# A with K and B: one load and one set of transposes for each pair of chunks, and a new plan of the order

## The chip, the cores and the metric

The kernel runs on one core of a Trainium2 chip. The metric is device time in microseconds (us) of one execution, the median of three runs: 961.42 us before the change (956.11 to 964.44).

## The reference

Two things are computed one after the other: a recurrence over 768 steps with a 40 x 40 state for each of 4 x 8 heads, and an MLP across tokens and then across channels.

```python
B, H, S, D = 4, 8, 768, 40
for t in range(S):
    y[:, :, t] = einsum('bhd,bhde->bhe', r[t], state)
    Sa = einsum('bhde,bhe->bhd', state, a[t])
    state = state * w[t][:, :, None, :] - einsum('bhd,bhe->bhde', Sa, b[t]) \
            + einsum('bhd,bhe->bhde', v[t], k[t])
x = y.transpose(0, 2, 1, 3).reshape(B, S, H * D)
u = x + (relu(x.T @ w_tok1) @ w_tok2).T        # 768 -> 256 -> 768, each batch
out = u + relu(u @ w_ch1) @ w_ch2              # 320 -> 1536 -> 320
```

## The kernel before

The steps are cut into chunks of 64. A batch has 12 chunks, all of its 8 heads at once (two heads of a pair p lie in the two row halves of a tile), so there are 48 chunks, numbered through; most steps work on two neighbouring chunks, a chunk pair. The recurrence inside a chunk becomes a triangular system, which is solved, and the state goes from chunk to chunk through small matmuls.

- `t_prep`: a batch comes in four quarters of 16 steps of every chunk (`pin`, four loads of w, a, k, b). A scan (`CP`), a reciprocal (`rq`, `RC`) and some products give the decayed K, B, A and P, which are stored to DRAM as `sKB`, `sA` and `sP`.
- The A phase. `t_a` loads K and B of a chunk, all heads side by side, into `KBa` (two buffers) and A into `AT` (rows: head half and step); `t_a2` loads A of a chunk pair a second time, into the one buffer `A2`. Transposes on TensorE (`pk`, `pa`, helper L265) and copies give `KBT` and `ATB`, and `t_px` multiplies them (`px`, 16 matmuls a pair, L643) into the chunk matrices: `Dg`, `N21`, and the lower part of `AT`.
- `t_solve` (VectorE) inverts the 32 x 32 diagonal blocks of eight chunks at a time by steps of `tmp` and `Tl`, with results `TBt` and `TBn`; it runs six times. `merge` (`pm`) joins blocks, `t_b` (`pe`, `pt`, `ph`) makes `HU` of a pair.
- `t_load` and `t_v` bring v and r (`W2s`, transposed as `pv`), `t_chain` runs the recurrence (`pq`, `pr`, `pS`, `pU`: L1119, L1141, L1146, L1200 on), `t_y` the output (`yb`).
- `t_piece` cuts the MLP's weights into pieces (`cv_t` for the token weights, `cv_c` for the channel weights), splits each into two parts and stores them to `sT` and `sG`; `t_mlp` loads these (`wg`, on GpSimd's queue) and has five matmul stages a batch, m1 to m5 (L1638, L1528).
- While TensorE waits, `filler` (L358) multiplies an identity into a tile that nobody reads; 42 such matmuls stand at the start as a warm-up.

No loop order stands in the code. Each step is a generator that yields lists of instructions with an estimated duration, and `Planner` lays them out on a modelled clock: whenever an engine is free, the ready instruction of the lowest rank goes next, and fillers go where TensorE's modelled queue would idle. The ranks come from the table `K` (`a`, `prep`, `solve`, `mlp`, ...). The outcome is one fixed list for each engine, and on the chip every engine runs its list in order. A `Ring` hands out buffers: who needs one waits in the plan until it is given back, and on the chip the instruction waits for the last reader. The DMA queue of SyncE (SP) is such a list too: a load whose buffer is still in use holds up all loads behind it. Helpers record many operations under one line (L374 for most DMAs, L265 for transposes), so names are to be read with the lines.

Of the kernel before, what the change touches and what calls it, by code (L numbers as in the profile page):

```python
# [38 lines left out]
class Ring:  # L39
# [6 lines left out]
    @property  # L46
    def free(self):
        return not self.taken[self.given % self.n]
# [19 lines left out]
class Planner:  # L68
# [5 lines left out]
    TICK, ENTRY = 10240 / 3, 3300.0  # L74
# [22 lines left out]
    def rel(self, ring, now, slot=None):  # L97
        ring, slot = ring if isinstance(ring, tuple) else (ring, slot)
        ring.give(slot)
        while ring.queue and ring.free:  # L100
            ring.queue.sort(key=lambda x: (x[1][1], x[0]))
            _, t = ring.queue.pop(0)
            ring.take()
            self.step(t, max(t[2], now))

    def step(self, t, now):
        t[2] = now
        send = now
        while True:
# [17 lines left out]
            if isinstance(cmd, Ring):  # L127
                if not cmd.free or cmd.queue:
                    self.seq += 1
                    cmd.queue.append((self.seq, t))  # L130
                    return
                cmd.take()
                continue
# [22 lines left out]
    def clock(self, t0, ns, cols, form):  # L156
# [7 lines left out]
        return sw + (ns if self.cols.get(i - 1, 0.0) >= self.ENTRY else 2 * ns)  # L164

    def fill(self, t0):
# [14 lines left out]
        self.free["PE"] = now + self.clock(now, ns, 192.0, "A")  # L181
# [58 lines left out]
def tile_kernel(ctx, tc, r, k, v, w, a, b, wt1, wt2, wc1, wc2, out, dbg=None):  # L240
# [89 lines left out]
    sA = [tc.dram_tile([H, NC, C, D], F32, name=f"sA{i}") for i in range(B)]  # L330
# [16 lines left out]
    def bank(tag, shape, name):  # L347

        ring = PQ[tag]
        yield ring  # L350
        return ps.tile(shape, F32, tag=tag, name=name, bufs=K[tag]), (ring, ring.last)

# [32 lines left out]
    def t_prep(bi):  # L385
# [9 lines left out]
        for q in range(NQ):  # L395
# [10 lines left out]
            def load(i, src, q=q, d=d, ring=ring, tsl=tsl):  # L406
# [5 lines left out]
                return ("SP", (480.0, 683.0), f)  # L412

            def comp(q=q, d=d, ring=ring, tsl=tsl):
# [80 lines left out]
                def rest():  # L495
# [4 lines left out]
                    now = yield [dma(lambda: sKB[bi].rearrange("h c (w t) e -> (h c) w t e", w=2)[:, :, tsl], lambda: pin[:, 2:4], 650.0, 1365.0)]  # L500
# [9 lines left out]
                    dma(lambda: sA[bi].rearrange("h c t e -> (h c) t e")[:, tsl], lambda: A),  # L510
                    dma(lambda: sP[bi].rearrange("h c t e -> (h c) t e")[:, tsl], lambda: W)]
# [48 lines left out]
    R_at, R_kbt = Ring(ATN), Ring(2)  # L560
    R_kbas, R_atbs = [Ring(1) for _ in range(2)], [Ring(1) for _ in range(2)]
# [25 lines left out]
    ab_ready = [Event() for _ in range(NG)]  # L587
    R_a2 = Ring(1)

    def t_a2(g, rank):  # L590

        bi, c = divmod(g, NC)
        early = g < SETS[0]
        d = {}
        yield R_a2

        src = sA[bi].rearrange("(p h) c t e -> h c t p e", h=2)
# [3 lines left out]
        a2f = A2.rearrange("p h e -> p (h e)")  # L601

        def pa(p):
            def f():
                transp(d["pa"][0:DP, p, :], a2f[:, p * 128:p * 128 + DP], ident)
            return ("PE", (109, 256, "A"), f)
        for z in range(2):
            yield R_atbs[z]
        d["pa"], tk = yield from bank("c" if early else "w", [128, NP, 128], f"pa{g}")
        now = yield [pa(p) for p in range(NP)]  # L610
        P.rel(R_a2, now)

        def abc(z):
            o_, i_ = ATB[z], d["pa"][0:DP, :, z * 64:z * 64 + 64]
            if g < K["ea"]:
                return ("DVE", 420, lambda: nc.vector.tensor_copy(out=o_, in_=i_))
            return ("ACT", 380, lambda: nc.scalar.copy(out=o_, in_=i_))
        for z in range(2):
            now = yield [abc(z)]
            P.set(ab_ready[g + z], now)  # L620
        P.rel(tk, now)

    k_ready, x_done_ = [Event() for _ in range(NG)], [Event() for _ in range(NG)]

    def t_px(g, tag, rank):

        for z in range(2):
            yield ab_ready[g + z]
            yield k_ready[g + z]
        yield Dg_free[SETOF[g][0]]  # L630
        yield Dg_free[SETOF[g + 1][0]]
        bk = []
        for z in range(2):
            x = yield from bank(tag, [128, NP, 128], f"px{g + z}")
            bk.append(x)
# [1210 lines left out]
```

## Time and profile before

| What | Value |
|---|---|
| median of three runs | 961.42 us (956.11 to 964.44) |
| span of the profiled execution | 963.6 us |
| PE, matmuls | 846.3 us (88%), x14452 |
| PEld, weight loads | 761.9 us (79%) |
| DVE | 615.5 us (64%), x1533 |
| ACT | 530.9 us (55%), x1432 |
| POOL | 222.7 us (23%), x311 |
| DMAs on SP's queue by the program | 752, of which the A phase's loads are 240 |
| DMA bytes | 149.77 MB |

PE is busy for most of the span, but evenly only in its second half: the mean over the whole says little of where time can be won. A busy PE at a granted clock below 1 does its work at less than full speed. The DMA queue is shared by all loads and stores of SP; what counts there is which transfer an engine waits for.

### The profile page before, as it was taken

To read this page: it belongs to the slowest core of one execution; us is meant where nothing else is said; L and a number is where in the kernel's file an instruction comes from. 1 tells how busy PE (TensorE), PEld (TensorE's weight loads), DVE (VectorE), ACT (ScalarE), POOL (GpSimd) and SP (SyncE) were. 2 spreads that over 40 slices of the span, in tenths; PEclk is the share of its full clock that TensorE was granted. 3 is DMA by queue.
4 is the path that set the end of the run, shared out by engine and by line. 5 is a ranking of instruction groups with operands and counts; after the bars stand their busy time and mean duration, and the time that the engine had idled before them with its cause. 6 is when DMAs were issued, how large, how long until landed. Compare 5 with 4: busy or idle time off the path is not lost.

```text
span 963.6 us, 34457 instructions
## 1 busy us (share of the span) xinstructions
PE 846.3 (88%) x14452; PEld 761.9 (79%) x14452; DVE 615.5 (64%) x1533; ACT 530.9 (55%) x1432; POOL 222.7 (23%) x311
## 2 busy tenths in 40 slices
PE   2766756889989968699999999999999999999997
PEld 2655645768878857588889888999889898999997
DVE  7547767587757779457984489543895535354443
ACT  4255645677676757386677564556546445443221
POOL 6111236332534325131341011101121110000000
PEclk7888865577786778799999979999999999999999
DMA  7599776688776797937764937456337443255522
GB/s 204 149 178 197 170 185 173 182 200 191 189 184 154 177 253 194 227 65 172 183 176 76 232 97 190 93 130 146 75 97 215 136 120 75 81 138 154 181 90 86
DMA packets 271729, 149.77 MB, mean 155 GB/s; under 512 B 232528, under 2 KB 249680, under 8 KB 268496
## 3 DMA queue, kind: packets, MB, share of 16 engines
q1 hardware_dynamic: 265232, 100.31, 46.2%
q0 software_dynamic: 6336, 47.19, 15.1%
q8 instruction: 116, 1.90, 0.9%
q14 instruction: 45, 0.37, 0.1%
HBM read 113.05 MB, written 34.41 MB: 153 GB/s over the span
## 4 chain that ended last, share of the span: by engine, by line
PE 60%; DMA 14%; DVE 12%; ACT 5%; SPq 5%; issue 3%; POOL 0%; DVEq 0%; ACTq 0%; POOLq 0%
PE m L1528 17%; PE m L1638 14%; DMA KBa<-sKB 3%; PE pq L1146 3%; SPq L374 3%; PE pq L1119 2%; DMA cv_c<-in_moe_w_ch_dram 2%; PE pe L996 2%; PE pt L1025 2%; PE ph L1049 2%; DMA W2s<-in_r_dram 2%; PE pq L1141 2%; PE px L643 2%; PE yb L1261 2%; PE yb L1263 2%
## 5 line engine op out<-in xcount | busy, mean ns | idle before, releaser
L1638 PE MATMUL m<-ut,wg_c 128*128 128x256 f32 x1152 | 175.9, 294 | 2.3 <-DVE x L1678 2.2
L1638 PEld LDWEIGHTS m<-ut,wg_c 128*128 128x128 f32 x1152 | 150.9, 192 | 9.2 <-DVE x L1678 3.0
L1528 PE MATMUL m<-wg_c,hd 128*128 128x320 f32 x864 | 152.8, 320 | 1.6 <-DVE hd L1650 1.5
L1528 PEld LDWEIGHTS m<-wg_c,hd 128*128 128x128 f32 x864 | 129.9, 191 | 6.2 <-DVE hd L1650 2.6
L1648 ACT ACTIVATE hd<-m 128x256 fp32r<-128x256 f32 x144 | 55.4, 385 | 125.6 <-PE m L1638 124.2
L1650 DVE SCALAR_TENSOR_TENSOR hd<-m,hd 128x256 fp32r<-128x256 f32 x144 | 60.6, 422 | 79.6 <-ACT hd L1648 78.9
L1678 DVE TENSOR_TENSOR x<-m,x 128x320 f32<-128x320 f32 x96 | 46.8, 488 | 74.2 <-PE m L1528 73.9
L371 POOL TENSOR_TENSOR cv_c<-cv_c 128x320 f32<-128x320 f32 (+3 forms) x56 | 56.7, 1020 | 65.8 <-ACT cv_c L1364 51.7
L358 PE MATMUL yb<-ident 128*128 128x192 bf16 x530 | 67.0, 283 | 2.0 <-POOL ident masks.py:199 1.8
L728 ACT ACTIVATE Dg<-px 128x128 f32<-128x128 f32 x144 | 55.9, 388 | 22.8 <-PE px L643 14.5
L358 PEld LDWEIGHTS <-ident 128*128 128x128 bf16 x530 | 53.2, 113 | 7.2 <-POOL ident masks.py:199 1.8
L1463 POOL DMA_DIRECT2D wg_c<-sG x32 | 17.8, 556 | 158.0 <-PE m L1638 79.2
L371 POOL TENSOR_TENSOR pin<-pin,RC 96x640 f32<-96x640 f32 x18 | 32.2, 1796 | 91.7 <-DVE RC L479 53.6
L1155 POOL TENSOR_TENSOR RM<-G,upp 64x128 f32<-64x128 f32 x34 | 17.6, 526 | 152.5 <-ACT G L1136 143.5
L1261 PE MATMUL yb<-KB,RM 128*64 128x40 f32 x768 | 51.1, 238 | 0.0
L1263 PE MATMUL yb<-VSs,RBs 104*64 104x40 f32 x768 | 50.7, 237 | 0.0
L1235 ACT COPY VSs<-pU 40x160 f32<-40x160 f32 x88 | 25.1, 285 | 45.3 <-PE pU L265 44.1
L265 PE MATMUL pv<-ident,W2s 128*104 128x128 f32 x192 | 33.5, 294 | 16.6 <-DMA W2s<-in_r_dram 16.3
L265 PE MATMUL pk<-ident,KBa 128*104 128x128 f32 x192 | 36.3, 312 | 12.3 <-DMA KBa<-sKB 11.6
L1261 PEld LDWEIGHTS yb<-KB,RM 128*64 128x64 f32 x768 | 44.7, 148 | 0.6 <-issue 0.2
L1263 PEld LDWEIGHTS yb<-VSs,RBs 104*64 104x64 f32 x768 | 44.6, 147 | 0.0
L693 ACT COPY KBT<-pk 104x512 f32<-104x512 f32 x48 | 28.2, 587 | 27.5 <-PE pk L265 26.8
(203 smaller groups left out, 1979.0 us busy)
## 6 DMA issues: line engine op xcount, KB each, us to landing
wg_c<-sG POOLq DMA_DIRECT2D x16, 1152.0 KB, 6.1
wg_c<-sG POOLq DMA_DIRECT2D x16, 960.0 KB, 5.4
wg_t<-sT POOLq DMA_DIRECT2D x8, 1280.0 KB, 6.5
sKB<-pin SPq DMA_DIRECT2D x16, 480.0 KB, 4.0
KB<-sKB SPq DMA_DIRECT2D x48, 160.0 KB, 3.8
sG<-cv_c SPq DMA_DIRECT2D x24, 192.0 KB, 3.7
pin<-in_w_dram SPq DMA_DIRECT2D x16, 240.0 KB, 4.4
pin<-in_a_dram SPq DMA_DIRECT2D x16, 240.0 KB, 5.6
```

The lines of the kernel that those rows point to most:

```text
L265: nc.tensor.matmul(out_, lhsT=in_, rhs=idn, start=True, stop=True, is_transpose=True)
L358: nc.tensor.matmul(yb[:, 320:512], lhsT=zf[:, 0:128], rhs=zf[:, 0:192], start=True, stop=True)
L371: return [(e, Port(60 + f * n / 0.96 if e == "DVE" else 140 + 2.24 * n), lambda e=e: engines[e].tensor_tensor(out=out_(), in0=a_(), in1=b_ ...
L374: return ("SP", (ns, data), lambda: nc.sync.dma_start(out=dst(), in_=src()))
L728: return ("ACT", 190 if sl.start == 0 else 392, lambda: nc.scalar.activation(out=Dg[sl, :, ci * NP:(ci + 1) * NP].rearrange("p s n -> p n s"),
L1261: nc.tensor.matmul(dst, lhsT=rms[g - 1 + z][:, h, :], rhs=o["kb"][:, h, :], start=True, stop=False)
L1263: nc.tensor.matmul(dst, lhsT=o["rb"][:, h // 2, q0:q0 + 64], rhs=o["vs"][:, h // 2, 64:DP], start=False, stop=True)
L1528: nc.tensor.matmul(d[key], lhsT=lhs(i, a_), rhs=rhs(i, b_), start=i == 0 and j == 0, stop=i == n - 1 and j == 2)
L1638: nc.tensor.matmul(pt, lhsT=mm_[q][0], rhs=mm_[q][1], start=q == 0, stop=q == len(mm_) - 1)
L1648: nc.scalar.activation(out=hid[key][:, 0], in_=pt, func=AF.Relu)
L1650: now = yield [("DVE", dve(256), lambda: nc.vector.scalar_tensor_tensor(out=hid[key][:, 1], in0=pt, scalar=0.0, in1=hid[key][:, 0].bitcast ...
L1678: now = yield [("DVE", dve(320), lambda: tt(out=x()[:, i], in0=d[("c2", g, i)], in1=x()[:, i], op=ALU.add))]
```

## The change

A of a pair is loaded once. `t_a2`, `t_px` and the first half of `t_a` give way to `t_ab`, which handles a pair from its loads to `px`. K and B of both chunks go side by side into one buffer `KBp` of 128 x 8 x 2 x 64 (one buffer for two `KBa`), so a transpose of one head brings chunk z into row half z. A goes into a fixed tile of `AT` for the pair (six for thirteen single ones), of which a transpose takes heads q into column half q; `px` then takes its row half by the chunk and its column half by the head. A pair issues four DMAs, where it issued ten. `sA` is laid out with the chunk outermost, and the copy to `ATB` is one of 512 columns for a pair. Banks and ring slots can be taken two at a time (`banks`, `Ring.free(n)`). In the planner the estimated durations are written anew, and so are a few ranks of `K` and the price of a filler and of matmuls at the lower clock (`HALF`, `ENTRY`).

```diff
-K = dict(..., atn=13, ld=7.33, ..., slack_c=800, ..., b=1.98, ..., mrg=3.19, ..., warm=42, ..., prep=[-15.86, ...], ..., mlp=[11.7, 24.73, 34.3, 41.82], ...)
+K = dict(..., atn=6, kbp=1, ld=6.75, ..., slack_c=560.87, ..., b=2.06, ..., mrg=3.17, ..., warm=37, ..., prep=[-15.76, ...], ..., mlp=[11.72, 24.75, 34.32, 41.84], ...)
...
-    TICK, ENTRY = 10240 / 3, 3300.0
+    TICK, ENTRY = 10240 / 3, 3350.0
+    HALF = {"A": 1.93, "B": 1.85, "C": 1.92, "D": 1.05}
...
-        return sw + (ns if self.cols.get(i - 1, 0.0) >= self.ENTRY else 2 * ns)
+        return sw + (ns if self.cols.get(i - 1, 0.0) >= self.ENTRY else self.HALF[form] * ns)
...
-        self.free["PE"] = now + self.clock(now, ns, 192.0, "A")
+        self.free["PE"] = now + self.clock(now, ns, 236.0, "A")
...
-    KBa = zbufs([128, H, 64], "KBa", 2)
-    ATB = zbufs([DP, NP, 64], "ATB", 2)
-    A2 = zbufs([128, H, 64], "A2", 1)[0]
+    AW = DP + 128
+    KBp = zbufs([128, H, 2, 64], "KBp", K["kbp"])
+    ATs = [ctile([128, NP, AW], f"AT{i}") for i in range(ATN)]
...
-    sA = [tc.dram_tile([H, NC, C, D], F32, name=f"sA{i}") for i in range(B)]
+    sA = [tc.dram_tile([NC, H, C, D], F32, name=f"sA{i}") for i in range(B)]
...
-                return ("SP", (480.0, 683.0), f)
+                return ("SP", (520.0, 800.0), f)
...
-    def t_a2(g, rank):
...
-        yield [dma(lambda: A2[0:64, :, 0:D], lambda: sA[bi][:, c].rearrange("h s e -> s h e"), 480.0, 228.0)] + [
-            dma(lambda h=h: A2[64:128].rearrange("t (p h) e -> t p h e", h=2)[:, :, 1 - h, 0:D], lambda h=h: src[h, c + 1], 480.0, 114.0)
-            for h in range(2)]
...
+    def t_ab(g, rank):
...
+        yield prep_done[bi]
+        yield R_kbp
+        kbp = KBp[R_kbp.last]
+        yield R_at
+        at = ATs[R_at.last]
...
+        yield [dma(lambda z=z: kbp[:, :, z, 0:D], lambda z=z: sKB[bi][:, c + z].rearrange("h s e -> s h e"), 620.0, 960.0) for z in range(2)] + [
+               dma(lambda z=z: at[:, :, z * 64:z * 64 + D],
+                   lambda z=z: sA[bi][c + z].rearrange("(p q) t e -> (q t) p e", q=2), 655.0, 480.0) for z in range(2)]
...
+                    transp(pk[0:DP, h % 4], kbp[:, h].rearrange("p z e -> p (z e)")[:, 0:DP], ident)
...
+                transp(pa[0:DP, p], at[:, p, 0:DP], ident)
...
+            d["atb"] = ap_.tile([DP, NP, 128], F32, tag="ATB", name=f"ATB{g}", bufs=1)
...
                 for q in range(2):
                     for z in range(2):
-                        r0, c0 = q * 64, (q ^ z) * 64
-                        nc.tensor.matmul(bk[z][0][c0:c0 + 64, p, :], lhsT=ATB[z][r0:r0 + D, p, :],
-                                         rhs=st[g + z]["kbt"][r0:r0 + D, p, :], start=True, stop=True)
-            return ("PE", (250, 400, "C"), f)
+                        h = 2 * p + q
+                        nc.tensor.matmul(bk[z][0][q * 64:q * 64 + 64, p, :], lhsT=d["atb"][z * 64:z * 64 + D, p, q * 64:q * 64 + 64],
+                                         rhs=ks[h // 4][z * 64:z * 64 + D, h % 4, :], start=True, stop=True)
+            return ("PE", (218, 60, "C"), f)
...
     def t_a(g, rank):
...
-            yield [dma(lambda: kba[:, :, 0:D], lambda: sKB[bi][:, c].rearrange("h s e -> s h e"), 480.0, 910.0), lat(0), lat(1)]
...
-                return ("PE", (36, 16, "D"), f)
+                return ("PE", (16, 32, "D"), f)
...
-                return ("PE", (190, 832, "B"), f)
+                return ("PE", (178, 626, "B"), f)
...
+            if g % 2 == 0:
+                P.spawn(t_ab(g, ra), ra)
...
-            P.filler = (K["fill"] * 1e3, 80.0, K["fill_cols"], filler)
+            P.filler = (K["fill"] * 1e3, 83.0, K["fill_cols"], filler)
```

The order moves on every engine. On SP, right after the stores of the first batch's prep, the ten loads of the first pair stood ahead of the loads of the second batch's prep (`pin1`):

```order
L374 DMA A20_118<-sA0_156 64x8x40
L374 DMA A20_118<-sA0_156 64x4x40 x2
L374 DMA KBa0_110<-sKB0_152 128x8x40
L672 DMA AT0_441<-sA0_156 64x4x40 x2
L374 DMA KBa1_111<-sKB0_152 128x4x40 x2
L672 DMA AT1_470<-sA0_156 64x4x40 x2
L411 DMA pin1_0_479<-in_w_dram 96x640
L411 DMA pin1_0_479<-in_a_dram 96x640
L411 DMA pin1_0_479<-in_k_dram 96x640
L411 DMA pin1_0_479<-in_b_dram 96x640
```

In the changed kernel the pair has four loads there, and the four of `pin1_0`, the four of `pin1_1` and one of `pin1_2` follow, with the second pair's `KBp` behind them:

```order
L388 DMA KBp0_110<-sKB0_156 128x8x40 x2
L388 DMA AT0_112<-sA0_160 128x4x40 x2
L425 DMA pin1_0_454<-in_w_dram 96x640
L425 DMA pin1_0_454<-in_a_dram 96x640
L425 DMA pin1_0_454<-in_k_dram 96x640
L425 DMA pin1_0_454<-in_b_dram 96x640
L425 DMA pin1_1_468<-in_w_dram 96x640
L425 DMA pin1_1_468<-in_a_dram 96x640
L425 DMA pin1_1_468<-in_k_dram 96x640
L425 DMA pin1_1_468<-in_b_dram 96x640
L425 DMA pin1_2_490<-in_w_dram 96x640
L388 DMA KBp0_110<-sKB0_156 128x8x40 x2
```

Nine loads of the second batch's prep now stand between the first pair and the second.

On DVE the first solve starts with the transpose `DT0`. Before, the third quarter of the second batch's prep (`CP1_2`, `rq1_2`, `RC1_2`) was threaded through its first steps:

```order
L769 STREAM_TRANSPOSE DT0_935<-Dg0_120 128x32x32
L444 COPY D1_101<-CP1_1_740 96x40
L450 SCALAR_TENSOR_TENSOR CP1_2_962<-W1_102,D1_101 96x680
L791 TENSOR_TENSOR tmp0_1_979<-Tl0_107,DT0_935 128x2
L793 TENSOR_REDUCE Tl0_107<-tmp0_1_979 128x2
L791 TENSOR_TENSOR tmp0_2_985<-Tl0_107,DT0_935 128x8
L793 TENSOR_REDUCE Tl0_107<-tmp0_2_985 128x2x2
L464 TENSOR_SCALAR rq1_2_991<-ce1_545 96x80
L483 RECIPROCAL rq1_2_991<-rq1_2_991 96x80
L791 TENSOR_TENSOR tmp0_3_1003<-Tl0_107,DT0_935 128x18
L477 TENSOR_TENSOR RC1_2_1006<-rq1_2_991,CP1_2_962 96x2x40
```

Now a token weight's piece (`cv_t2_1_0`) and the copy of the fifth pair (`ATB8`) stand there:

```order
L748 STREAM_TRANSPOSE DT0_1080<-Dg0_124 128x32x32
L385 TENSOR_TENSOR pin1_3_578<-pin1_3_578 96x640
L770 TENSOR_TENSOR tmp0_1_1125<-Tl0_107,DT0_1080 128x2
L656 COPY ATB8_1127<-pa8_1096 104x512
L772 TENSOR_REDUCE Tl0_107<-tmp0_1_1125 128x2
L1333 TENSOR_SCALAR cv_t2_1_0_1005<-cv_t2_1_0_1005 128x384
L770 TENSOR_TENSOR tmp0_2_1142<-Tl0_107,DT0_1080 128x8
L1334 SCALAR_TENSOR_TENSOR cv_t2_1_0_1005<-cv_t2_1_0_1005 128x384
L772 TENSOR_REDUCE Tl0_107<-tmp0_2_1142 128x2x2
L1336 TENSOR_SCALAR cv_t2_1_0_1005<-cv_t2_1_0_1005 128x384
L770 TENSOR_TENSOR tmp0_3_1163<-Tl0_107,DT0_1080 128x18
```

The prep has gone ahead of the solve, and weight pieces, which need a load of their own, came in.

On PE the recurrence starts with `pq0` (the last of its first matmuls is the first row here), and `pq0 <- G0, HU0` is its second part. Before, px of the seventh pair (chunks 12 and 13) followed at once:

```order
L1119 MATMUL pq0_1_1923<-RBs0_136,VSs0_142 40x64
L947 MATMUL pm6_1816<-TBn0_1323,ET10_122 32x32 x9
L358 LDWEIGHTS ident_79
L358 MATMUL yb_166<-ident_79 128x192
L1141 MATMUL pq0_1_1923<-G0_895,HU0_1870 64x104 x4
L1141 MATMUL pq0_0_1922<-G0_895,HU0_1870 64x104 x4
L643 MATMUL px12_2011<-KBT12_1473,ATB0_114 64x128
L643 MATMUL px13_2012<-KBT13_1978,ATB1_115 64x128
```

Now the transposes of that pair (`pk12`) stand there, ahead of a filler:

```order
L1005 MATMUL pt2_2036<-ET2_1986,TBn0_1451 32x32 x5
L1115 MATMUL pq0_1_1981<-G0_686,HU0_1928 64x104 x4
L1115 MATMUL pq0_0_1980<-G0_686,HU0_1928 64x104 x4
L271 MATMUL pk12_0_1969<-ident_79,KBp0_110 104x128 x4
L372 LDWEIGHTS ident_79
L372 MATMUL yb_170<-ident_79 128x192
```

px of chunks 12 and 13 has moved behind the next chunk's pq. Counted over PE's whole list, fillers go from 530 to 693: from 416 to 503 ahead of pq0, from 79 to 167 between pq0 and the first matmul of the MLP (36 of them in one row just ahead of it), from 35 to 23 behind it.

## Rows read from the trace of the kernel before

**Rows 1.** Busy time by stretches of the span; columns in the first line.

```profile
core 0: us, PE busy (x) PEld busy (x) DVE busy (x) ACT busy (x) POOL busy (x), PEclk, DMA share, GB/s
0.00:41.00 41.00, 18.24 (x148) 17.80 (x149) 30.69 (x74) 17.13 (x25) 18.36 (x39) 0.75 0.67 192
41.00:163.00 122.00, 78.93 (x1390) 66.69 (x1390) 81.71 (x201) 63.90 (x134) 33.27 (x29) 0.77 0.77 172
163.00:373.00 210.00, 184.36 (x4048) 159.63 (x4045) 151.42 (x352) 143.66 (x383) 79.62 (x92) 0.72 0.79 195
373.00:600.00 227.00, 210.30 (x3641) 188.66 (x3637) 158.48 (x408) 141.68 (x401) 56.10 (x85) 0.94 0.66 155
600.00:870.00 270.00, 266.76 (x4554) 242.90 (x4544) 154.14 (x407) 142.30 (x425) 30.11 (x57) 1.00 0.47 121
```

**Rows 2.** Chain that ended last, in order of time: start us, us, what.

```profile
37.11 3.79 DMA sA<-pin
...
162.37 1.06 PE pq L1119 x30
...
373.39 3.14 PE m L1528 x20
```

**Rows 3.** Chain that ended last: shares by engine, then by line.

```profile
PE 60%; DMA 14%; DVE 12%; ACT 5%; SPq 5%; issue 3%; POOL 0%; DVEq 0%; ACTq 0%; POOLq 0%
...
by line: PE m L1528 17.0%; PE m L1638 13.6%; DMA KBa<-sKB 3.2%; issue 3.1%; PE pq L1146 2.7%; SPq L374 2.6%; PE pq L1119 2.4%; DMA cv_c<-in_moe_w_ch_dram 2.2%; PE pe L996 2.1%; PE pt L1025 2.0%; PE ph L1049 1.9%; DMA W2s<-in_r_dram 1.9%; PE
```

**Rows 4.** SP's queue in order of time: start us, us, what, how many.

```profile
40.92 1.98 SPq L374 DMA_DIRECT2D A<-sA  x3
42.94 0.61 SPq L374 DMA_DIRECT2D KBa<-sKB  x1
...
46.09 1.24 SPq L672 DMA_DIRECT2D AT<-sA  x2
```

**Rows 5.** Waits of SP's queue: us in total, times, longest us.

```profile
SPq L374 <- PE pk L265: 30.1, 10, 11.7
SPq L672 <- PE ph L1049: 24.1, 8, 9.4
...
SPq L374 <- PE pa L265: 18.9, 6, 10.6
```

**Rows 6.** DVE's timeline around the first solve; in brackets the idle time before.

```profile
99.94 0.42 DVE L616 COPY ATB<-pa 104x256 f32<-104x256 f32 x1 [3.14 <-PE pa L265]
...
105.94 0.20 DVE L464 TENSOR_SCALAR rq<-ce 96x80 f32<-96x80 f32 x1 [2.05 <-ACT ce L460]
...
130.81 1.99 DVE L450 TENSOR_TENSOR_SCAN CP<-W,D 96x680 f32<-96x680 f32 x1 [1.13 <-ACT W L433]
137.54 0.36 DVE L1359 TENSOR_SCALAR cv_t<-cv_t 128x384 int32<-128x384 int32 x1 [4.75 <-DMA cv_t<-in_moe_w_tok_dram]
137.82 0.27 DVE L959 TENSOR_TENSOR TBt<-pm,TBt 128x64 f32<-128x64 f32 x1
```

**Rows 7.** Groups of instructions by line: count | busy us, mean ns | idle before.

```profile
L358 PE MATMUL yb<-ident 128*128 128x192 bf16 x530 | 67.0, 283 | 2.0 <-POOL ident masks.py:199 1.8
...
L643 PE MATMUL px<-KBT,ATB 40*64 40x128 f32 x768 | 36.0, 319 | 6.6 <-ACT KBT L693 5.1 <-ACT PCt L535 1.5
```

**Rows 8.** PE's timeline: one run of px and one of pm.

```profile
78.60 1.42 PE L643 MATMUL px<-KBT,ATB 40*64 40x128 f32 x32
...
121.47 0.68 PE L947 MATMUL pm<-ET,TBn 32*32 32x32 f32 x32 [0.81 <-DVE ET L954]
```

**Rows 9.** PE's longest wait from 373 to 600 us: total, times, longest.

```profile
PE pv L265 <- DMA W2s<-in_r_dram: 8.0, 2, 7.7
```

**Rows 10.** DMA issues: count, KB each, median us from issue to landing.

```profile
sKB<-pin SPq DMA_DIRECT2D x16, 480.0 KB, 4.0
...
sA<-pin SPq DMA_DIRECT2D x16, 240.0 KB, 3.7
```

**Rows 11.** Chain from 250 to 373 us, shares by line.

```profile
by line: PE pq L1141 9.1%; DMA KBa<-sKB 8.7%; DMA cv_c<-in_moe_w_ch_dram 7.9%; issue 5.1%; PE yb L358 4.5%; PE pv L265 4.1%; PE pq L1119 4.0%; PE ph L1049 3.9%; DMA W2s<-in_r_dram 3.5%; DMA sG<-cv_c 2.8%; PE pe L996 2.7%; DMA P<-sP 2.7%; PE
```

More of the change, by code (lines that the diff above doesn't have):

```diff
@@ L44, in __init__, with free @@
         self.out = []
-    @property
-    def free(self):
-        return not self.taken[self.given % self.n]
+    def free(self, n=1):
+        return not any(self.taken[(self.given + i) % self.n] for i in range(n))
     def take(self):
@@ L99, in rel @@
         ring.give(slot)
-        while ring.queue and ring.free:
+        while ring.queue:
             ring.queue.sort(key=lambda x: (x[1][1], x[0]))
-            _, t = ring.queue.pop(0)
-            ring.take()
+            _, t, n = ring.queue[0]
+            if not ring.free(n):
+                return
+            ring.queue.pop(0)
+            for _ in range(n):
+                ring.take()
             self.step(t, max(t[2], now))
@@ L126, in step @@
                 continue
-            if isinstance(cmd, Ring):
-                if not cmd.free or cmd.queue:
+            if isinstance(cmd, (Ring, tuple)):
+                ring, n = cmd if isinstance(cmd, tuple) else (cmd, 1)
+                if not ring.free(n) or ring.queue:
                     self.seq += 1
-                    cmd.queue.append((self.seq, t))
+                    ring.queue.append((self.seq, t, n))
                     return
-                cmd.take()
+                for _ in range(n):
+                    ring.take()
                 continue
@@ L351, in bank, with banks @@
         return ps.tile(shape, F32, tag=tag, name=name, bufs=K[tag]), (ring, ring.last)
+    def banks(tag, shape, names):
+        ring = PQ[tag]
+        yield ring, len(names)
+        return [(ps.tile(shape, F32, tag=tag, name=n, bufs=K[tag]), (ring, (ring.last - len(names) + 1 + i) % ring.n)) for i, n in enumerate(names)]
     yb = ps.tile([128, 512], F32, tag="y", name="yb", bufs=1)
@@ L604, in f @@
             def f():
-                transp(d["pa"][0:DP, p, :], a2f[:, p * 128:p * 128 + DP], ident)
+                transp(pa[0:DP, p], at[:, p, 0:DP], ident)
             return ("PE", (109, 256, "A"), f)
-        for z in range(2):
[L608 to L635, printed above, removed]
+        yield [paf(p) for p in range(NP)]
@@ new lines, in atb @@
+        def atb():
+            d["atb"] = ap_.tile([DP, NP, 128], F32, tag="ATB", name=f"ATB{g}", bufs=1)
+            if g < K["ea"]:
+                nc.vector.tensor_copy(out=d["atb"], in_=pa[0:DP])
+            else:
+                nc.scalar.copy(out=d["atb"], in_=pa[0:DP])
+        now = yield [("DVE", dve(512), atb) if g < K["ea"] else ("ACT", act(512), atb)]
+        P.rel(tk, now)
+        for z in range(2):
+            yield Dg_free[SETOF[g + z][0]]
+        bk = yield from banks(tg[2], [128, NP, 128], [f"px{g}", f"px{g + 1}"])
@@ L684, in t_a @@
-        d = {}
-        def pk(p):
-            def f():
-                transp(d["pk"][0:DP, p, :], kbf[:, p * 128:p * 128 + DP], ident)
-            return ("PE", (109, 256, "A"), f)
-        def kbt():
-            d["kbt"] = ap_.tile([DP, NP, 128], F32, tag="KBT", name=f"KBT{g}", bufs=2)
-            nc.scalar.copy(out=d["kbt"], in_=d["pk"][0:DP])
-        yield R_kbt
-        d["pk"], tk = yield from bank(tg[0], [128, NP, 128], f"pk{g}")
-        yield [pk(p) for p in range(NP)]
-        now = yield None
@@ L1329, in t_piece @@
         yield A_loaded[min(K["conv_after"], NG - 1)]
-        ring = R_big if R_big.free and not R_wg.free and not mlp_on else R_wg
+        ring = R_big if R_big.free() and not R_wg.free() and not mlp_on else R_wg
         yield ring
```

158 lines of the change are left out of this document (73 added, 85 removed).

## The prediction

> **What bounds the kernel now.** The table by stretches comes first, because a mean over 963.6 us hides three regimes [rows 1]. Up to 41 us TensorE has almost nothing to do (18.24 us busy). [...] From 373 to 600 us it is 210.30 of 227 us busy at 0.94, and from 600 us to 870 it is 266.76 of 270 at 1.00: there only a cheaper matmul shortens anything. So time can be won ahead of 373 us, where the first MLP matmuls start [rows 2], and little after it. The chain that ended last says the same: 60% PE, but 14% DMA landings, 12% DVE and 5% SP's issuing [rows 3], and the last three lie mostly in the first 373 us.
>
> Next, the SP queue in order of time. From 40.92 to 47.33 us it does nothing but issue the ten loads of the first chunk pair, at about 0.6 us each [rows 4]. Then the waits of that queue: it stood 18.9 us for pa to free the one A2 buffer, 30.1 us for pk to free KBa and 24.1 us for ph to free AT [rows 5]; each time every load behind it stood as well. Last, DVE's own timeline around the first solve: it idles 3.14 us ahead of an ATB copy, 2.05 us ahead of rq, 1.13 us ahead of the scan of prep 2 and 4.75 us ahead of a weight piece [rows 6]. That last wait holds a merge's TBt, so the recurrence, whose first pq runs at 162.37 us [rows 2].
>
> **The change part by part.**
>
> *SP issues.* Ten DMAs per pair become four (two KBp, two AT): 6 x 24 = 144 of 752 issues go, and A crosses once instead of twice (160 KB less per pair, 3.84 of 149.77 MB). At 0.6 us that is 86 us of the queue's time, 50 us of it ahead of the MLP (14 of 24 pairs). Most of this isn't on the path. The chain gives SP 5% of 963.6 us = 48 us; with 144/752 = 19% of the issues gone the proportional share is 9 us. Ends: 0 if what follows on SP waits for buffers anyway, and 25 us, the whole 2.6% that the chain books on the loads' helper line L374 [rows 3]. I take **-9**, because the order puts other work in the gap: the eight loads of prep 1's first two quarters and W2s come forward to where A2 and AT stood, so KBp of the second pair still queues behind nine 240 KB loads.
>
> *DVE around the first solve.* Before, prep 1's third and fourth quarter are threaded through the solve; now they are done ahead of it and five weight pieces (cv_t) are threaded through instead. The stalls of [rows 6] between 96 and 138 us are 3.14 + 2.05 + 1.13 + 4.75 = 11.1 us. If all vanish, -11; if the pieces inside the solve wait for their loads as the one at 137.54 did, two such waits cost +10. I take **-5**: about half goes, since the merges no longer have a fresh load just ahead of them, while ATB of the fifth pair still waits for its KBp inside the solve.
>
> *px.* The same 16 matmuls per pair, but the row half now changes at every matmul (z picks the row, q the column), where two neighbours shared it. 36.0 us in all [rows 7]. No row shows this shape in the new order. Ends: 0, and the pace of the merges' matmuls, which step through the row groups: 0.68 against 1.42 us for 32 records [rows 8], hence 36.0 x (1 - 0.68/1.42) = 19 us less, for a quarter of the columns. The diff writes 218 for 250 into the plan, 13%; I take that, **-4.6**, much nearer to zero since px streams 128 columns. [...]
>
> *Landings that PE waits for after 373 us.* pv waits 8.0 us in two pieces for W2s [rows 9]. In the new order pv of chunk 17 stands behind the first three MLP tiles and pq16 instead of ahead of them, so W2s has that much longer to land. Ends 0 and -8; **-3**, as other loads still share the queues with the big weight loads.
>
> *The store of A.* sA's layout puts chunks outermost, so the store's destination reads 8x12x640 where it was 96x640. The last such store of prep 0 lies on the chain for 3.79 us [rows 2]. Ends 0 and +3.8 (all of it twice); sKB with twice the bytes lands in 4.0 against 3.7 us [rows 10], so bytes are a small part: **+0.3**. [...]
>
> *Fillers.* 530 become 693 by the order: 87 more before pq0, 88 more between pq0 and the first MLP matmul (79 before), 12 fewer after it. Each is 67.0/530 = 0.126 us of PE [rows 7]. The first 87 fall in a stretch where PE idles 122 - 79 = 43 us [rows 1] and cost nothing while it does; 11 us stand if that cover is gone. Of the 88, at most 11 us are on the path; before, fillers were 4.5% of the chain from 250 to 373 us [rows 11], 5.5 us or half of what they took there. Against that stands a higher clock in a stretch that has 0.72. Ends: +11 and -25 (last rival). I take **+3**.
>
> *At nothing:* the five fewer memsets and six small new ones (GpSimd, before 41 us, under prep 0's DMA and DVE work); 24 ATB copies of 512 columns for 48 of 256 (ACT is 143.66 of 210 us busy, and idle enough afterwards); five fewer warm-up matmuls, in a stretch where PE waits 20 us; AT's ring of 12 chunks for 13, since the second batch's first pair waits for ph of the first pair either way. If ACT or that ring were the last to be waited for, each would show as one wait of the sort in [rows 5], 1 to 3 us.
>
> Sum: -9 - 5 - 4.6 - 3 + 0.3 + 3 = -18.3 us, and 963.6 - 18.3 = 945.3 us. The profiled execution lies 2.2 us above the median of the three runs (961.42; 956.11 to 964.44), so the forecast is 945.3 - 2.2 = **943 us**, and its own range, with the middle halves of the bounds, 933 to 953.
>
> **The rivals.**
>
> *Washed out, 958 us.* The front gets shorter but the first MLP matmul doesn't start sooner, because it waits for weight pieces and x0, and the recurrence runs behind in the in-order queue of PE. For it: 36 fillers stand in one row just ahead of that matmul, a place where the plan itself expects to wait. Against: the pieces come earlier in SP's order than before. Left are px and W2s: 961.4 - 4.6 - 3 + 3 = 957, say 958.
>
> *Slower, 973 us.* DVE stalls inside the first solve. Five pieces stand between its steps; the last ones can be loaded only after an earlier piece is stored and its buffer given back, and SP issues that store in order behind AT and prep 1's stores. Each such wait is a 4.75 us one, and the whole recurrence (pq0) is behind it. Three waits in the first solve give +14, and TBt reaches pe late. It decides from the second wait on: with one, the stalls that go still pay for it. 961.4 + 14 - 4.6 - 3 + 5 (no stall gained, some fillers on the path) = 973. For it: the wait at 137.54 us was of this kind. Against: the pieces start earlier.
>
> *The clock, 922 us.* The fillers hold the clock up from 163 to 373 us. At the 0.94 of the next stretch, 184.36 us of PE work would be 184.36 x 0.72/0.94 = 141 us, plus 11 us of fillers: 32 us less, bounded by DVE's 151 us and the chain of ACT and DVE between the matmuls, so about -25. Then 961.4 - 25 - 14 (SP and DVE terms) = 922. Against: in that stretch 79 fillers did not do it, and half of the added ones stand in two rows of 13 and 16 and one of 36.
>
> **How the numbers follow.** Forecast 0.50, washed out 0.23, slower 0.17, clock 0.10. Range 922 to 973: it leaves out a tenth at either end, roughly. The three runs of the kernel before span 0.9%, so 1% is about what a measurement can tell from no change. Faster by over 1% means under 951.8: most of the forecast's case (0.46) and the clock's (0.10), 0.56. Slower by over 1%, over 971.0: most of the slower case and the tail of the second, 0.17. The rest, 0.27, is within.
>
> **What would show it.** Right: SP's timeline from 41 to 100 us with gaps; no wait for pa on SP; pq0 at 150 to 157 us; the first MLP matmul at 355 to 362 us; px under 32 us in all; after 600 us PE as busy as now. Wrong: pq0 at 162 us or later, waits of DVE for cv_t between the solve's steps, or the first MLP matmul at 370 us again in spite of an earlier pq0 (then the weights set it); a clock over 0.85 from 163 to 373 us would speak for the last rival. What I can't read from the trace is how the many small waits of five in-order queues add up under a new order; that alone can move the time by the 1% either way.

## The result and the profile after

The changed kernel took 946.88 us (median of five runs, 946.75 to 954.88) against 962.90 for the kernel before (956.11 to 971.50, also five): a ratio of 0.987, 95% interval 0.983 to 0.991. The forecast was 943 us with a range of 922 to 973. The profiled execution was the slowest of the five (span 953.2 us), so a second profile of the same kernel (span 947.7 us; run `same_again` below) is read beside it wherever a few us count.

Starts of the first matmul of a stage, read from the three traces (us):

| | before | after | again |
|---|---|---|---|
| first ph | 151.2 | 151.2 | 148.6 |
| pq of chunk 0, first part | 162.3 | 156.1 | 153.1 |
| pq of chunk 0, second part (needs G and HU) | 164.2 | 162.0 | 159.4 |
| first MLP block | 373.3 | 361.3 | 357.5 |
| second | 578.7 | 560.4 | 553.9 |
| third | 737.9 | 726.8 | 719.0 |
| fourth | 875.6 | 864.9 | 858.7 |

So the first part of pq0 runs 6 to 9 us earlier, 12 to 16 us are won by the first MLP block and 6 to 9 more by the second; 6 to 7 of them are given back ahead of the third. Of the 6 to 9 us, some 4 are only a matter of order: the first part now stands ahead of other matmuls, and the second part, without which the recurrence doesn't go on, comes 2 to 5 us earlier. PE's timeline before, after and again:

```profile
164.17 3.04 PE L1141 MATMUL pq<-G,HU 104*64 104x104 f32 x16
```

```profile
161.99 3.03 PE L1115 MATMUL pq<-G,HU 104*64 104x104 f32 x16
```

```profile
159.40 3.04 PE L1115 MATMUL pq<-G,HU 104*64 104x104 f32 x16
```

The stretches of [rows 1] in the profile after (columns as there):

```profile
0.00:41.00 41.00, 16.64 (x130) 16.25 (x131) 31.95 (x74) 17.12 (x25) 19.30 (x41) 0.71 0.65 181
41.00:163.00 122.00, 86.45 (x1631) 76.55 (x1629) 82.72 (x208) 67.97 (x140) 50.10 (x41) 0.81 0.82 196
163.00:373.00 210.00, 186.56 (x4155) 160.01 (x4153) 155.97 (x370) 149.76 (x392) 74.61 (x85) 0.85 0.73 182
373.00:600.00 227.00, 213.32 (x3723) 188.83 (x3725) 153.49 (x408) 139.09 (x389) 49.17 (x73) 0.96 0.64 150
600.00:870.00 270.00, 262.87 (x4394) 239.91 (x4395) 147.43 (x396) 139.39 (x418) 29.61 (x56) 0.99 0.47 120
```

PE is about as busy in each of them; its clock from 163 to 373 us is 0.85 instead of 0.72. That looks like the last rival, and an experiment has to tell whether it is. After 600 us PE now idles 7 us where it idled 3.

The groups of [rows 7], the chain's shares by engine [rows 3] and its landing of the A store [rows 2], in the same profile:

```profile
L372 PE MATMUL yb<-ident 128*128 128x192 bf16 x693 | 80.7, 274 | 3.8 <-DVE P L1267 2.0 <-POOL ident masks.py:199 1.8
...
L670 PE MATMUL px<-KBT,ATB 40*64 40x128 f32 x768 | 31.1, 301 | 12.4 <-DVE ATB L656 6.1 <-DVE rq L478 2.7 <-DVE fl L560 2.7
```

```profile
PE 59%; DMA 14%; DVE 12%; issue 6%; ACT 6%; SPq 3%; POOL 0%; DVEq 0%; ACTq 0%; POOLq 0%
```

```profile
38.25 5.53 DMA sA<-pin
```

px takes 31.1 us for 36.0, SP's issues 3% of the chain for 5%, fillers 80.7 us for 67.0, and the store of A lands in 5.53 us where it took 3.79. SP's queue in order of time [rows 4]:

```profile
42.14 1.03 SPq L388 DMA_DIRECT2D KBp<-sKB  x2
43.79 1.05 SPq L388 DMA_DIRECT2D AT<-sA  x2
44.89 0.49 SPq L425 DMA_DIRECT2D pin<-in_w_dram  x1
...
50.05 1.78 SPq L388 DMA_DIRECT2D KBp<-sKB  x2
51.88 5.79 SPq L388 DMA_DIRECT2D AT<-sA  x2
```

The first pair costs 2 us of the queue where it cost 6. The second pair's two AT issues take 5.79 us, though (5.41 in `same_again`). What holds them isn't shown: the issue right behind, of 240 KB at 57.71 us, took 0.50 us again. SP's waits for ph to free AT, over the whole span:

```profile
SPq L388 <- PE ph L1029: 48.5, 6, 28.5
```

The waits for pa are gone, but those for ph have doubled (24.1 us before, 9.4 at the longest [rows 5]; 40.6 in `same_again`), and 31 of the 48.5 us lie between the first and the second MLP block. DVE around the first solve [rows 6]:

```profile
80.36 0.36 DVE L1333 TENSOR_SCALAR cv_t<-cv_t 128x384 int32<-128x384 int32 x1 [3.86 <-DMA cv_t<-in_moe_w_tok_dram]
...
99.80 1.96 DVE L748 STREAM_TRANSPOSE DT<-Dg 128x1024 f32<-128x1024 f32 x1
...
126.21 0.36 DVE L1333 TENSOR_SCALAR cv_t<-cv_t 128x384 int32<-128x384 int32 x1 [0.79 <-issue]
...
127.78 1.96 DVE L826 STREAM_TRANSPOSE TBt<-Tl 128x1024 f32<-128x1024 f32 x1
```

The weight pieces inside the solve hardly wait (under 1 us each), and the merges have no stall of 4.75 us. But the solve starts at 99.80 us, 14 us later than before (85.7), since prep's third and fourth quarter stand ahead of it, and the first ph runs at the same 151 us. What is won inside the solve is lost again by its later start.

### The profile page after: what moved, and what is told of

Read it like the earlier page. It is cut to its first block, busy times and chain, and to the rows that moved or that the text cites. A ratio compares the mean times of both kernels' runs of the same rounds, so it can differ in the third digit from the quotient of the medians.

```text
span 953.2 us, 34564 instructions
## 1 busy us (share of the span) xinstructions
PE 843.6 (89%) x14605; PEld 758.2 (80%) x14605; DVE 607.1 (64%) x1538; ACT 531.0 (56%) x1412; POOL 227.0 (24%) x304
## 4 chain that ended last, share of the span: by engine, by line
PE 59%; DMA 14%; DVE 12%; issue 6%; ACT 6%; SPq 3%; POOL 0%; DVEq 0%; ACTq 0%; POOLq 0%
PE m L1502 15%; PE m L1612 13%; DMA W2s<-in_r_dram 4%; PE pm L927 3%; SPq L388 3%; PE pq L1095 2%; PE pq L1120 2%; PE pt L1005 2%; PE pv L271 2%; PE ph L1029 2%; DMA cv_t<-in_moe_w_tok_dram 2%; PE yb L372 2%; PE px L670 2%; PE pq L1115 2%; PE pe L976 2%
## 5 line engine op out<-in xcount | busy, mean ns | idle before, releaser
L372 PE MATMUL yb<-ident 128*128 128x192 bf16 x693 | 80.7, 274 | 3.8 <-DVE P L1267 2.0
L372 PEld LDWEIGHTS <-ident 128*128 128x128 bf16 x693 | 66.1, 109 | 10.0 <-issue 4.0
L271 PE MATMUL pv<-ident,W2s 128*104 128x128 f32 x192 | 32.9, 289 | 19.5 <-DMA W2s<-in_r_dram 16.9
L970 POOL COPY TBD<-TBt 32x256 f32<-32x256 f32 x33 | 22.2, 673 | 111.2 <-PE ph L1029 85.8
L1235 PE MATMUL yb<-KB,RM 128*64 128x40 f32 x768 | 48.0, 230 | 0.0
L385 POOL TENSOR_TENSOR pin<-pin,RC 96x640 f32<-96x640 f32 x19 | 33.8, 1787 | 59.4 <-DVE RC L493 38.1
L1237 PE MATMUL yb<-VSs,RBs 104*64 104x40 f32 x768 | 47.6, 229 | 0.0
L271 PE MATMUL pk<-ident,KBp 128*104 128x128 f32 x192 | 35.2, 301 | 12.3 <-DMA KBp<-sKB 12.3
L1235 PEld LDWEIGHTS yb<-KB,RM 128*64 128x64 f32 x768 | 40.8, 137 | 1.7 <-issue 0.8
```

The costliest lines, as they stand in the source:

```text
L271: nc.tensor.matmul(out_, lhsT=in_, rhs=idn, start=True, stop=True, is_transpose=True)
L372: nc.tensor.matmul(yb[:, 320:512], lhsT=zf[:, 0:128], rhs=zf[:, 0:192], start=True, stop=True)
L385: return [(e, Port(60 + f * n / 0.96 if e == "DVE" else 140 + 2.24 * n), lambda e=e: engines[e].tensor_tensor(out=out_(), in0=a_(), in1=b_ ...
L1235: nc.tensor.matmul(dst, lhsT=rms[g - 1 + z][:, h, :], rhs=o["kb"][:, h, :], start=True, stop=False)
L1237: nc.tensor.matmul(dst, lhsT=o["rb"][:, h // 2, q0:q0 + 64], rhs=o["vs"][:, h // 2, 64:DP], start=False, stop=True)
```

## The experiments

Three sets of four kernels; each set ran beside the kernel before on one chip, six to twelve executions of each kernel. A time is the median; a ratio is to the kernel before, with its 95% interval. Traces are of one execution each: pq0 and the MLP blocks are read from it, and a few us between two traces can be chance.

**1. same_again**: the changed kernel, no edit.

> The changed kernel once more, unchanged. Its profiled execution took 8 us more than the other four, and in it TensorE idled 8 us from 560 to 727 us, behind a load of x. If that wait was a matter of one execution, a second profile shows 945 us and the load of x ends no wait. If it is in the order, it is there again and the time is 947 all the same. Either way 945 to 949 us.

949.08 us, 0.987 (0.982 to 0.992). The wait is there again, in the chain of waits of this profile:

```profile
690.74 8.24 DMA sX<-P
699.00 5.61 DMA x<-sX
704.63 0.47 ACT sp L1462
```

and in its waits of PE from 554 to 719 us:

```profile
PE pU L271 <- ACT VSs L1209: 4.0, 1, 4.0
```

So it belongs to the order: x of a batch goes through DRAM, ACT's next instruction in order waits for it, and the copies to VSs of the recurrence stand behind that. The kernel before had no such wait (PE idled 3 us from 579 to 738 us; 8 us here from 554 to 719).

**2. no_mid_fill**: the changed kernel without the 167 fillers between pq0 and the first MLP matmul; all other instructions in the same order.

```diff
+FILL0, FILL1 = 503, 670
...
+    nfill = [0]
+
     def filler():
+        nfill[0] += 1
+        if FILL0 < nfill[0] <= FILL1:
+            return
         nc.tensor.matmul(yb[:, 320:512], lhsT=zf[:, 0:128], rhs=zf[:, 0:192], start=True, stop=True)
```

> The 167 fillers between pq0 and the first MLP matmul are left out, all else in the same order. Theory of the clock: the granted clock of that stretch falls from about 0.83 to the 0.72 of before or lower, the stretch grows by 6 us or more, and the time is 953 to 962 us. Theory that fillers are load without use: 19 us less work for TensorE there, half of it on the path, 936 to 942 us. If they only fill gaps: 945 to 949 us at an unchanged clock.

951.36 us, 0.987 (0.982 to 0.991), the same as with them. The stretch from pq0 to the first MLP block of this kernel:

```profile
156.00:360.00 204.00, 170.53 (x4009) 146.99 (x4001) 145.67 (x360) 146.28 (x387) 74.54 (x83) 0.77 0.77 185
```

and of `same_again`:

```profile
153.00:358.00 205.00, 176.56 (x4195) 151.83 (x4184) 144.48 (x359) 147.49 (x391) 75.37 (x84) 0.85 0.75 186
```

The clock falls, as the theory of the clock has it, and the stretch keeps its length, which it excludes. Over the whole span, PE without fillers is busy 838.1 - 58.9 = 779.2 us here and 840.1 - 79.0 = 761.1 us in `same_again` (762.9 in the profile after): some 16 to 18 us of matmuls that run slower, against 20 us of fillers that are gone. These 167 fillers pay for themselves and for no more.

**3. ten_issues**: the changed kernel with each pair's four loads cut into ten, at their places in the order and with the same bytes; every engine but SP has the same list.

```diff
+        def ld_kb(z):
+            for h0, h1 in ((0, 3), (3, 6), (6, 8)):
+                nc.sync.dma_start(out=kbp[:, h0:h1, z, 0:D], in_=sKB[bi][h0:h1, c + z].rearrange("h s e -> s h e"))
+        def ld_at(z):
+            for q in range(2):
+                nc.sync.dma_start(out=at[q * 64:q * 64 + 64, :, z * 64:z * 64 + D],
+                                  in_=sA[bi][c + z].rearrange("(p q) t e -> q t p e", q=2)[q])
```

> Each pair's four loads are cut into ten, as many as before, of the same bytes in all and at the same places of the order. Theory that SP's issues were the cost: 144 issues come back, the first MLP matmul starts 5 us later or more, and the time is 953 to 960 us, 9 us of it by the proportional share. Rival that the queue waits for buffers anyway: pq0 and the first MLP matmul stand within 2 us of where they are, 946 to 949 us.

977.35 us, 1.016 (1.011 to 1.021): 28 us more than `same_again` on the same chip, three times the forecast's share, and 1.6% or 15 us more than the kernel before, which issues as many. pq0 starts at 167.6 us for 153.1, the first MLP block at 381.7 for 357.5, the second at 587.5 for 553.9. From there it loses nothing more (390 us to the end of the span, 394 in `same_again`). SP's queue at the first two pairs of this kernel:

```profile
41.66 3.04 SPq L620 DMA_DIRECT2D KBp<-sKB  x6
44.74 2.62 SPq L624 DMA_DIRECT2D AT<-sA  x4
...
51.87 6.01 SPq L620 DMA_DIRECT2D KBp<-sKB  x6
```

The loads behind them move back step by step: the third load of r into `W2s` is issued at 68.57 us for 63.68, the ninth of b into `pin` at 128.66 for 117.36. That fits a queue that has no slack. It doesn't separate the time of the issues from a later landing of a load in pieces; where KBp stands on the chain it lands in 3.7 and 4.7 us, in `same_again` in 3.9 to 4.9, so KBp shows no later landing. But pa waits 9.0 us for AT, five times, and in `same_again` not at all; whether AT's pieces are only issued later or also land later isn't shown.

**4. px_row_pairs**: the changed kernel with px's two inner loops exchanged, so that neighbours share the row half.

```diff
-                for q in range(2):
-                    for z in range(2):
+                for z in range(2):
+                    for q in range(2):
                         h = 2 * p + q
```

> px's loops are exchanged, so that two neighbours share the row half again; nothing else moves. Theory that the alternating row half makes px cheaper: px takes 35 to 37 us in all instead of 31.1, and the time is 949 to 952 us. Rival that px fell with the clock only: px stays at 30 to 32 us, the time at 945 to 949 us.

950.67 us, 0.990 (0.986 to 0.995): no difference from `same_again` that can be told, so the time doesn't decide between the two. px of this kernel (the trace is of an execution of 937.67 us), to set beside 31.1 and (again) 28.6 us:

```profile
L670 PE MATMUL px<-KBT,ATB 40*64 40x128 f32 x768 | 31.2, 302 | 12.9 <-DVE ATB L656 5.0 <-DVE fl L560 3.0 <-DVE rq L478 2.6
```

And px of `plan_alone` below, which has px's code of before, in row pairs, under the new plan:

```profile
L644 PE MATMUL px<-KBT,ATB 40*64 40x128 f32 x768 | 32.6, 294 | 1.4 <-issue 1.1 <-DVE ATB L617 0.2
```

In both, px in row pairs is nearly as cheap as in the changed kernel, so the order of the row halves isn't what made it cheaper. In `plan_alone` 3.4 of the 4.9 us come without any edit of px.

**5. six_dummies**: behind each of a pair's two AT loads three DMAs more.

```diff
+            for i in range(3):
+                nc.sync.dma_start(out=sD[g // 2, z, i], in_=ident[0:64, 0:2])
```

> The changed kernel with six further DMAs for each pair behind its loads, of 64 x 2 elements into a DRAM tile that nobody reads; loads and order stay as they are. Theory that the time of SP's queue for an issue is the cost: 144 issues cost about what the cut loads cost (28 us), 965 to 980 us. Rival that the cut loads landed later in ten pieces: 946 to 953 us.

1053.40 us, 1.101 (1.097 to 1.106): outside what either theory gave. The issues cost SP what AT's own cost, 0.6 us each, but AT's own landings stand on the chain five times up to 130 us, with 6.4 to 8.5 us each. In the changed kernel's chains there is one in the profile after (7.2 us at 517.6 us) and none in `same_again`; the median of the same 80 KB loads is known for `loads_alone` alone, 3.8 us. The issues of three of the small DMAs, and the first and last of the five landings:

```profile
42.96 1.79 SPq L622 DMA_DIRECT2D sD<-ident  x3
```

```profile
44.79 7.75 DMA AT<-sA
...
128.22 8.51 DMA AT<-sA
```

So these DMAs, of 512 bytes (64 x 2 elements) and by the profile 80 packets each, weren't cheap: PE's pa waits 17.1 us for AT (0.6 in the profile after, none in `same_again`). How they hold AT up isn't shown. As a price for an issue this run says nothing.

**6. at_on_pool**: AT's two loads issued by GpSimd.

```diff
-               dma(lambda z=z: at[...], lambda z=z: sA[bi][c + z]..., 655.0, 480.0) for z in range(2)]
+               ("SWD", (700.0, 480.0), lambda z=z: nc.gpsimd.dma_start(out=at[...], in_=sA[bi][c + z]...)) for z in range(2)]
```

> The two loads of A of each pair are issued by GpSimd instead of SP, and the planner lays the rest out anew with that. Theory that each issue taken off SP is worth 28/144 = 0.2 us: 48 issues, 9 us, 936 to 942 us. Rival that GpSimd's queue and its own work hold the loads up: 950 to 965 us, with waits of TensorE's pa for AT.

966.07 us, 1.005 (1.002 to 1.009): no gain. The planner laid all else out anew with it, so the run doesn't separate the queue from the order, and its stages are not compared.

**7. loads_alone** and **8. plan_alone**: the new code of the A phase with every duration, rank and filler price of before; and the code before with the new ones (t_load's rank stays). The first as a diff against the changed kernel, three of its numbers; the second is the same the other way round.

```diff
-                return ("SP", (520.0, 800.0), f)
+                return ("SP", (480.0, 683.0), f)
...
-                return ("PE", (16, 32, "D"), f)
+                return ("PE", (36, 16, "D"), f)
...
-            P.filler = (K["fill"] * 1e3, 83.0, K["fill_cols"], filler)
+            P.filler = (K["fill"] * 1e3, 80.0, K["fill_cols"], filler)
```

> The new code of the A phase with the durations, ranks and filler prices of before. Theory that the gain comes from the fewer issues: 945 to 953 us. Rival that the new plan was needed for it: 956 to 970 us.

> The kernel before with the new durations, ranks and filler prices, except the rank of t_load, with which its plan doesn't run to an end. Theory that the loads give the gain: 957 to 968 us, like before. Rival that the plan gives it: 940 to 953 us.

990.73 us, 1.034 (1.029 to 1.039), for the loads alone, and 967.34 us, 1.012 (1.008 to 1.016), for the plan alone. Neither half gives the gain; the loads without the plan cost more than twice what both together bring. With the loads alone pq0 starts at 169.8 us and the first MLP block at 409.9; PE idles 55.6 us between them (28.4 in `same_again`).

The plan alone does win the front: pq0 starts at 147.8 us and the first MLP block at 353.5, 20 us earlier than before and earlier than in the changed kernel. It loses that up to the second block (576.5 us; before, 578.7):

```profile
148.00:353.00 205.00, 180.39 (x4031) 156.02 (x4025) 140.34 (x340) 139.95 (x368) 76.30 (x87) 0.77 0.71 179
353.00:576.00 223.00, 203.44 (x3500) 179.43 (x3498) 155.04 (x395) 143.44 (x393) 57.09 (x75) 0.94 0.72 169
```

From the first to the second block it takes 223 us, where the kernel before takes 205 and the changed one 199. A part of that is order: without fillers, its list has 4966 matmuls ahead of the first block, the kernel before 5087 and the changed one 5108, and it has 110 to 120 more than these two between the blocks. An early first MLP matmul is thus no sure sign of an early end.

**9. late_pk**: the kernel before, with the four transposes pk of chunk 13 (the ones that wait for KBa ahead of pq0) behind the matmuls of pq0's first part (`late` keeps them back until these are out). ACT's copy of them to KBT is kept back with them; no other instruction moves.

```diff
-            return ("PE", (109, 256, "A"), f)
+            return ("PE", (109, 256, "A"), late(f) if g == 13 else f)
...
-            nc.scalar.copy(out=d["kbt"], in_=d["pk"][0:DP])
+            cp = lambda: nc.scalar.copy(out=d["kbt"], in_=d["pk"][0:DP])
+            (late(cp) if g == 13 else cp)()
```

> The kernel before; only the four transposes pk of chunk 13, which stand ahead of pq0 on TensorE and waited 4.7 us for their load, are put behind pq0's sixteen matmuls. Theory that this wait is where the changed kernel's recurrence starts earlier: pq0 starts 4 to 5 us earlier, its second part at least 2 us, and the time is 957 to 961 us if that lasts to the end. Rival that pq0's start isn't what the end follows: the first MLP matmul at 372 to 375 us as before, 961 to 965 us.

960.61 us, 1.000 (0.997 to 1.003). The load on the chain of the kernel before, PE's wait for it there, and PE's timeline of this kernel:

```profile
156.53 4.68 DMA KBa<-sKB
```

```profile
161.30 1.07 PE L265 MATMUL pk<-ident,KBa 128*104 128x128 f32 x4 [2.31 <-DMA KBa<-sKB]
```


```profile
160.75 1.13 PE L1125 MATMUL pq<-RBs,VSs 40*64 40x64 f32 x32
162.49 1.06 PE L265 MATMUL pk<-ident,KBa 128*104 128x128 f32 x4 [0.61 <-DMA KBa<-sKB]
163.48 0.53 PE L953 MATMUL pm<-TBn,ET 32*32 32x32 f32 x18
165.34 3.03 PE L1151 MATMUL pq<-G,HU 104*64 104x104 f32 x16 [1.07 <-ACT G L1146]
```

PE's wait for the load shrinks from 2.31 us to 0.61; the 4.7 us of the expectation are the load's landing, not PE's wait. pq0's first part starts 1.6 us earlier, though the first ph came 1.8 us later in this trace (153.0 us), and its second part (L1151) not at all: 165.34 against 164.17. Where PE waited for the load it now waits for ACT's G.

**10. old_ranks, 11. old_durations, 12. one_rank_b**: the changed kernel with the ranks of before (ld, slack_c, b, mrg, warm, prep, mlp); with the durations, HALF, ENTRY and filler price of before; and with one rank of before, of which this is the diff.

```diff
-         -5.24], solve_span=4.19, atomic=0, a=10.07, a_span=3.08, b=2.06, chain=-0.25, evac=0.43, y=-0.77, utr=5.3,
+         -5.24], solve_span=4.19, atomic=0, a=10.07, a_span=3.08, b=1.98, chain=-0.25, evac=0.43, y=-0.77, utr=5.3,
```

> The changed kernel with the ranks of before (t_load, slack_c, t_b, merge, warm-up, prep, mlp) and the new durations and filler prices. Theory that the durations are what the new loads needed: 945 to 955 us. Rival that the ranks are: 965 to 990 us, like the loads alone. If any other order costs some per cent against the chosen one, the time lies anywhere between, and above 950.

> The changed kernel with the durations and filler prices of before, and the new ranks. Theory that the durations are what the new loads needed: 965 to 990 us. Rival that the ranks are: 945 to 955 us.

> The changed kernel with one rank of before, that of t_b (1.98 for 2.06, in chunks). Theory that a rank that moves by less than a tenth of a chunk leaves the time: 945 to 951 us. Rival that the time hangs on the one order found for it: 955 us or more, with the start of the first MLP matmul or the stretch behind it longer by as much.

956.22 us, 0.995 (0.991 to 0.998), with the old ranks; 983.54 us, 1.024 (1.020 to 1.028), with the old durations; 951.39 us, 0.990 (0.987 to 0.994), with the one old rank, no difference from the changed kernel that can be told. The durations (with the filler price and the factors at the lower clock) are what the new loads need; the ranks are worth some 0.7% beside them. In `old_durations` the stretch from pq0 to the first MLP block grows to 236 us with 51 us of idle PE:

```profile
172.00:408.00 236.00, 185.13 (x4137) 157.87 (x4136) 154.40 (x372) 150.05 (x384) 74.06 (x85) 0.77 0.72 168
```

The longest waits of PE in it are these (in `same_again` from 153 us to the first block, the first is 6.4 us, the second 2.4):

```profile
PE pv L271 <- DMA W2s<-in_r_dram: 10.4, 4, 8.5
PE pS L1174 <- DVE RM L1151: 7.7, 4, 4.2
PE pU L271 <- ACT ce L474: 6.9, 1, 6.9
```

No single wait makes up the 23 us by which PE idles more; which duration of the plan leads to them isn't shown.

## Why the prediction was right, and which of its terms were not

The time (943 forecast, 946.88 measured), the side and the places were right: pq0 at 156.1 us (150 to 157 forecast, some 4 us of it only the order in PE's list), the first MLP block at 361.3 (355 to 362), px 31.1 (under 32), no wait for pa on SP. The sum came out right over terms that were not: its largest was three times too small, one of much the same size was missing, and the two errors nearly cancel. That the number fits so well is luck; that the loads were worth cutting isn't.

- **SP issues, -9 us: three times too small.** In one and the same order, that of the changed kernel, six issues more per pair cost 28 us (`ten_issues`), beyond even the end of 25 that the prediction took from L374's share. A likely reason, not shown by itself: the chain books as issues only those that stand on it, while each issue also moves back every load behind it in the queue (5 us at 64 us, 11 at 117), and what waits for these is booked as DMA, DVE or PE. The waits for A2 that the prediction read in [rows 5] weren't what could be won ahead of the MLP: 16.2 of their 18.9 us lie between 361 and 560 us.
- **What ate the rest of it.** With ten loads a pair the new plan is slower than the old one, by 1.2% in the old code (`plan_alone`) and 1.6% in the new (`ten_issues`): 12 to 15 us. So -28 and +12 to +15 give the 12 to 16 us that were won (with the 15 this says nothing new, since both numbers come from `ten_issues`; the 12 is from a run of its own). The split holds for this order: under the old durations the new loads lose. The prediction had costed the new durations at nothing except where it saw the order move.
- **The plan as a term of its own was missing.** The loads and the plan are each a loss alone (+3.4% and +1.2%). With the old durations the new loads get an order in which PE idles 51 to 56 us where it idles 28. Which of the durations it is wasn't tried. The prediction also held that time can be won ahead of 373 us and little after it: `plan_alone` is 20 us ahead at that point and 2 us at the second block, and the changed kernel wins 6 to 9 us between the two.
- **DVE, -5 us: right that the stalls go, wrong in what follows.** They went, but the solve starts 14 us later, so the first ph didn't move (2.6 us in `same_again`). From ph to pq0's second part it is 10.8 us in both traces and was 13.0. KBa's landing (4.68 us) stood in the chain there before; `late_pk` shows that moving these transposes out of pq0's way, by itself, brings nothing, so that one place in PE's list isn't where the gain comes from. Where the 2 us come from stays open.
- **px, -4.6 us: right size, reason not borne out.** 31.1 and 28.6 us for 36.0. With the row halves in pairs px takes 31.2 us (`px_row_pairs`) and 32.6 (`plan_alone`), so the alternation isn't it. With one and the same code and order it is 34.1 us in `ten_issues` and 28.6 in `same_again`, so the 4.6 us are within what px moves by with the moment at which it runs. In `old_durations`, at a clock of 0.77 from 172 to 408 us, it is 33.8 us, in `no_mid_fill` at the same 0.77 it is 31.3: the clock of a whole stretch doesn't settle it either. In return the waits ahead of px rose from 6.6 to 12.4 us.
- **W2s, -3 us.** PE's waits for it from the first to the second MLP block are 5.9 us (8.0 before, [rows 9]): 2 us. Over the whole span they are as long as before (16.9 and 16.3 us).
- **The store of A, +0.3 us: too small.** 5.5 us for 3.8 at the same place of the chain, and 4.8 to 5.6 in the other runs of this layout whose chain holds it: +1.0 to +1.8, within the bound of 3.8.
- **Fillers, +3 us: 0.** 13.7 us more of them, at a clock that rose; `no_mid_fill` takes 167 away at no gain and no loss that can be told. The last rival had its sign in the profile (0.85) and not its gain: what the matmuls gained by the clock, the fillers took.
- **At nothing: AT's ring.** The prediction allowed one wait of 1 to 3 us. SP's waits for ph to free AT went from 24.1 to 40.6 and 48.5 us, 28 of them at one time. What they cost wasn't tried.
- **The rivals.** Slower: the pieces in the solve waited under 1 us each. Washed out: in part, and late, since 6 to 7 of the 18 to 25 us that were won by the second MLP block are given back in the stretch in which ACT waits for x (4.0 us of it by PE's wait in `same_again`). The sign "after 600 us PE as busy as now" failed by these: PE idles 7 us there for 3.

## What to carry to other kernels

In a kernel where one queue issues nearly all loads, put the issues back one for one in an unchanged order before believing a share of the critical path: here the share gave 9 us and the run 28. Where a planner lays out the instructions, a cheaper step and the durations that describe it are one change; either alone can cost more than the pair brings. A clock that rises under fillers is no gain until the stretch gets shorter: here it was 0.85 with 167 of them and 0.77 without, over 205 and 204 us. And a stage that starts earlier in a new order is no gain until the end does: `plan_alone` was 20 us ahead at the first MLP block and was no faster for it.

## What the runs showed of the hardware

The median issue on SP took 0.42 to 0.43 us for a load into `pin` (240 KB), 0.72 us for the store of A (240 KB), 0.59 us for KBp (160 KB) and 0.58 us for AT (80 KB) in the profile after, and 0.60 us for the 512 bytes of `six_dummies`; but two loads of AT took 5.79 us at 51.88 us. The small DMAs of `six_dummies`, 512 bytes and 80 packets each, cost 11.4% of the time of the kernel before, some 110 us, where as many cut loads cost 28; loads of AT beside them stood on the chain up to 130 us with 6.4 to 8.5 us. The store of A with the chunk outermost took 1.0 to 1.8 us longer to land than the same 240 KB did before (4.8 to 5.6 us for 3.8). The records of px's matmuls took 392 ns in the mean from 163 to 373 us of the kernel before, at a granted clock of 0.72, and 277 ns from 600 to 870 us, at 1.00.
